# Attention and two MoE layers on one core: two staging buffers in turns, one weight block made early instead of two

## The chip, the core and the metric

The kernel runs on one core of a Trainium2 chip. TensorE (PE) multiplies matrices, VectorE (DVE), ScalarE (ACT) and GpSimd (POOL) work on elements, and SyncE (SP) issues the DMAs. The metric is the device time of one execution in microseconds (us), the median of several runs.

## The reference, cut to what matters

Attention with 16 heads in all (2 batches of 8), 768 tokens each, 64 wide: a query sees only keys whose nearest centroid (of 16) is the same as its own. Its output, 1536 tokens of 512, goes through two layers, each two dense products with an activation between:

```python
x = attn_out.transpose(0, 2, 1, 3).reshape(1536, 512)
h = x @ w_in;  g = maximum(0.01 * h, h);  x = g @ w_out        # layer 1 (m = 0)
h = x @ w_in2; r = maximum(h, 0); g = r * r; out = g @ w_out2  # layer 2 (m = 1)
```

w_in is 512 x 2048 and w_out 2048 x 512 in both. The weights arrive as 64-bit floats in HBM.

## The kernel before, in words

**Precision.** Every float32 operand is split into a high part and a low part, and a product is made of three matmuls: high by high, high by low, low by high. The names end in h and l: `xh`, `xl` (input of a layer), `wh`, `wl` (weights), `gh`, `gl` (activated rows).

**Weight blocks.** A layer's 2048 inner columns are cut into 16 blocks (f), so there are 32 blocks in all, numbered ci. A block holds 128 columns of w_in and 128 rows of w_out, 1 MB of 64-bit words. `decode_pieces` (L114) makes its `wh` and `wl` in six pieces: `load` (one DMA into `wraw`, L121), `mag` (ScalarE into `wt`, L128), `shift`, `low` and `sign` (VectorE on `wt` in place, L132, L138, L145; the last two also read `wraw`) and `split` (ScalarE copies `wt` to `wh`, L156, and GpSimd writes `wl` = `wt` - `wh`, L157). `wraw` and `wt` are staging: a pool `stg` with one of each, opened at the start of attention's last pair (L678), and a second pool `stgb` with one of each, opened when attention's pools are closed (L712). In the kernel before, `stg[-1]` is the pool opened last, so blocks 0 and 1 go through the first one and all others, one after the other, through the second. The finished blocks lie in a ring of eight.

**Attention.** Eight pairs of heads, six units to a pair, 48 in all. A unit is 256 query rows: scores S on TensorE (L350), row maxima on VectorE (L373), exponentials `e` on ScalarE (L383), division on GpSimd (L400), transposes T on TensorE (L413, twelve to a unit), their split `eh`, `el` (L424, L430), the product A with the values (L448, twelve matmuls), and `xt` (L461, L470). After the last unit of a pair `xsplit` writes `xh` and `xl` (GpSimd, L162 and L478).

**The layers.** A unit of a layer is one block of 512 tokens (b, three of them) and one weight block f: g1 is 12 matmuls into an `h` bank of PSUM (L725), in four row blocks of three; `act` makes `gh` and `gl` from it (L738 to L746); g2 is 12 matmuls into four `o` banks (L767), two units later (LAG). The first group has blocks 0 and 1, its units run (b0,f0), (b0,f1), (b1,f0), (b1,f1), (b2,f0), (b2,f1). Token block 0 needs only the first batch; token blocks 1 and 2 need, in the last of the four row blocks, the last pair of heads.

**Order.** SP's queue is in program order throughout. The other engines follow a list written out by hand up to unit 41; from the last pair on (L682) a planner orders each engine's instructions, with the program order as priority. The pieces of the early blocks are handed out over the six units of the last pair (L700 to L704); those of the others at units of the layers that `plan` names (L800 to L817): a block of group n is made while the group before it runs, and those of the first two groups at unit 0 and after it.

Of the kernel before, what the change touches and what calls it, by code (L numbers as in the profile page):

```python
# [10 lines left out]
I32 = mybir.dt.int32  # L11
# [41 lines left out]
def attention_moe_moe_kernel(  # L53
# [14 lines left out]
    NT, DM = out.shape  # L68
# [7 lines left out]
    NBLK = NT // N  # L76
    G = 4
    GROUPS = ([2, 2] + [G] * (NF // G - 1), [G] * (NF // G))
    EARLY = 2
    RING = 8  # L80
    WARM = (9,4,10)

# [29 lines left out]
    stg = []  # L112

    def decode_pieces(ci):  # L114

        m, f = divmod(ci, NF)
        st = {}

        def load():
            st["raw"] = stg[-1].tile([128, 2 * DM, 2], I32, tag="wraw", name="wraw")  # L120
            nc.sync.dma_start(  # L121
                out=st["raw"].rearrange("p a b -> p (a b)"), in_=(w1, w2)[m][f].bitcast(I32)
            )

        def mag():
            t = stg[-1].tile([128, 2 * DM], I32, tag="wt", name="wt")
            st["t"] = t
            nc.scalar.mul(out=t.bitcast(F32), in_=st["raw"][:, :, 1].bitcast(F32), mul=W_SHIFT)  # L128

        def shift():  # L130
            t = st["t"]
            nc.vector.tensor_scalar(  # L132
                out=t, in0=t, scalar1=3, scalar2=None, op0=ALU.logical_shift_left
            )

        def low():
            t = st["t"]
            nc.vector.scalar_tensor_tensor(  # L138
                out=t, in0=st["raw"][:, :, 0], scalar=29, in1=t,
                op0=ALU.logical_shift_right, op1=ALU.bitwise_or,  # L140
            )

        def sign():
            t = st["t"]
            nc.vector.scalar_tensor_tensor(  # L145
                out=t, in0=st["raw"][:, :, 1], scalar=-0x80000000, in1=t,
                op0=ALU.bitwise_and, op1=ALU.bitwise_or,
            )

        def split():  # L150
            t = st["t"].bitcast(F32)
            pool = next(q for q, n in ring if ci % RING < n)
            wh = pool.tile([128, 2 * DM], F32R, tag="wh", name="wh")
            wl = pool.tile([128, 2 * DM], F32R, tag="wl", name="wl")
            weights[m, f] = (wh, wl)
            nc.scalar.copy(out=wh, in_=t)  # L156
            nc.gpsimd.tensor_tensor(out=wl, in0=t, in1=wh.bitcast(F32), op=ALU.subtract)  # L157

        return [load, mag, shift, low, sign, split]

    def pool_copy(out, in_):
# [510 lines left out]
    }  # L672

    early = [f for i in range(EARLY) for f in decode_pieces(i)]
    for u in range(-1, NU + 5):
        if u == NU - UPP:
# [7 lines left out]
        for op in PLAN[FIRST[u] if p == 0 else u % UPP].split():  # L684
            if ":" in op:
                name, lag = op.split(":")
# [5 lines left out]
            else:  # L692
                name, ahead = op.split("@")
# [107 lines left out]
    for m in range(2):  # L801
        f = 0
        for g, size in enumerate(GROUPS[m]):
            for i in range(size):
                if ci >= EARLY:
                    pcs = decode_pieces(ci)
                    at = last + i * (began - last) // size
                    n = max((began - last) // size, 1)
                    for k, pc in enumerate(pcs):
                        plan.setdefault(at + k * n // len(pcs), []).append(pc)  # L810
                ci += 1
            last = began
            for b in range(NBLK):
                for i in range(size):
                    units.append((m, b, f + i, g, i == 0, i == size - 1))
            began = len(units)
            f += size  # L817
# [60 lines left out]
```

## Time and profile before

| | |
|---|---|
| median of 3 runs | 793.64 us (792.76 to 794.53) |
| the profiled execution | 790.98 us, span 789.2 us |
| PE busy | 771.2 us (98% of the span) |
| DVE, ACT, POOL busy | 538.0, 412.7, 292.0 us |
| granted TensorE clock | 1.00 of full speed |

The span is from the first to the last instruction. An engine's busy time is the union of its instructions; matmuls are pipelined, so a busy PE says that something was always in it, not that it was at its peak. A chain of waits is followed back from the last instruction to whatever released each step.

### The profile page before, as it was taken

The page shows a single profiled execution, that of the slowest core. Times are in us where ns is not written, and L with a number is a line of the kernel's source. Part 1 is how long each engine was busy: PE and PEld are TensorE (multiplying, and loading weights), DVE is VectorE, ACT ScalarE, POOL GpSimd, SP SyncE. Part 2 cuts the span into 40 slices and gives each one's busy share as a digit, 9 for nine tenths or more (in the row PEclk, how much of TensorE's full clock was granted, in tenths as well). Part 3 has the DMA queues.
Part 4 walks back from the last instruction along what each step waited for, and adds up shares of the span by engine and source line. Part 5 has one row for each costly group of instructions (what it writes and reads, how often), then busy time and mean ns, then how long its engine had stood idle before and what let it go on. Part 6 is the DMA issues. An engine that isn't in the chain of part 4 may idle for free.

```text
span 789.2 us, 11011 instructions
## 1 busy us (share of the span) xinstructions
PE 771.2 (98%) x4147; PEld 664.4 (84%) x4147; DVE 538.0 (68%) x772; ACT 412.7 (52%) x759; POOL 292.0 (37%) x257
## 2 busy tenths in 40 slices
PE   8999999999989999999999999999999999999998
PEld 8899999999977778888888888888888888888886
DVE  5899999999997378876665568387356547533333
ACT  6988988988996464443432344345344334222221
POOL 2989889888854322122220124352022012100000
PEclk9999999999999999999999999999999999999999
DMA  7584574564510323123221022013112103000102
GB/s 222 120 205 108 109 173 116 113 153 91 125 54 2 107 106 107 60 100 108 107 107 54 1 106 82 26 54 108 54 53 107 54 0 108 1 0 1 45 23 94
DMA packets 16005, 66.35 MB, mean 84 GB/s; under 512 B 2704, under 2 KB 2704, under 8 KB 10960
## 3 DMA queue, kind: packets, MB, share of 16 engines
q1 hardware_dynamic: 15952, 65.64, 28.7%
q8 instruction: 33, 0.54, 0.3%
q14 instruction: 20, 0.16, 0.1%
HBM read 44.60 MB, written 3.15 MB: 60 GB/s over the span
## 4 chain that ended last, share of the span: by engine, by line
PE 81%; DVE 11%; ACT 4%; DMA 1%; issue 1%; POOL 1%; SPq 0%; DVEq 0%; ACTq 0%
PE o L767 33%; PE h L725 33%; PE A L448 5%; PE T L413 5%; PE S L350 5%; DVE el L430 3%; DVE nm L373 3%; ACT e L383 2%; DVE xt L470 1%; ACT eh L424 1%; DVE ds L276 1%; PE ohT L305 1%; DVE m L275 1%; DMA rqk<-qk 1%; DVE wt L138 1%
## 5 line engine op out<-in xcount | busy, mean ns | idle before, releaser
L157 POOL TENSOR_TENSOR wl<-wt,wh 128x1024 fp32r<-128x1024 f32 x32 | 76.8, 2400 | 292.6 <-ACT wh L156 235.6
L725 PE MATMUL h<-xh,wh 128*128 128x512 f32 x384 | 150.6, 393 | 2.2 <-DVE g L739 2.2
L725 PE MATMUL h<-xh,wl 128*128 128x512 f32 x384 | 150.6, 392 | 0.0
L725 PE MATMUL h<-xl,wh 128*128 128x512 f32 x384 | 150.5, 392 | 0.0
L746 DVE TENSOR_TENSOR gl<-g,gh 128x512 fp32r<-128x512 f32 x96 | 95.4, 994 | 47.6 <-ACT gh L745 47.5
L430 DVE TENSOR_TENSOR el<-T,eh 128x512 fp32r<-128x512 f32 x144 | 94.8, 683 | 7.8 <-ACT eh L424 6.0
L745 ACT CAST gh<-g 128x512 fp32r<-128x512 f32 x96 | 59.6, 621 | 73.0 <-DVE g L742 42.7
L400 POOL TENSOR_SCALAR e<-e,r 128x768 f32<-128x768 f32 x96 | 88.0, 927 | 20.1 <-DVE r L397 14.7
L373 DVE TENSOR_REDUCE nm<-S 128x1 f32<-128x768 f32 x96 | 90.7, 946 | 4.6 <-PE S L254 2.2
L350 PE MATMUL S<-hb 128*128 128x384 f32 (+1 forms) x384 | 90.6, 350 | 3.0 <-ACT e L383 2.6
L383 ACT ACTIVATE e<-S,nm 128x768 f32<-128x768 f32 x96 | 87.0, 906 | 11.7 <-DVE nm L373 7.4
L742 DVE TENSOR_TENSOR g<-t 128x512 f32<-128x512 f32 x48 | 39.4, 822 | 72.8 <-ACT t L741 72.7
L725 PEld LDWEIGHTS h<-xh,wh 128*128 128x128 f32 x384 | 72.2, 188 | 18.5 <-DVE g L739 2.6
L741 ACT ACTIVATE t<-h 128x512 f32<-128x512 f32 x48 | 28.7, 598 | 112.0 <-PE h L725 111.9
L424 ACT CAST eh<-T 128x512 fp32r<-128x512 f32 x144 | 79.6, 585 | 12.9 <-PE T L413 12.3
L725 PEld LDWEIGHTS h<-xh,wl 128*128 128x128 f32 x384 | 72.2, 188 | 16.0
L725 PEld LDWEIGHTS h<-xl,wh 128*128 128x128 f32 x384 | 72.2, 188 | 15.9
L448 PE MATMUL A<-eh,vv 128*128 128x256 f32 x288 | 79.5, 306 | 3.5 <-DVE xt L470 3.5
L413 PE MATMUL T<-ident,e 128*128 128x128 f32 x576 | 81.0, 274 | 1.1 <-DVE el L430 1.0
L738 ACT ACTIVATE t<-h 128x512 f32<-128x512 f32 x48 | 28.6, 598 | 95.6 <-PE h L725 95.6
L767 PE MATMUL o<-gh,wl 128*128 128x512 f32 x192 | 75.3, 392 | 0.0
L767 PE MATMUL o<-gh,wh 128*128 128x512 f32 x192 | 74.5, 393 | 0.8 <-DVE xt L470 0.8
(105 smaller groups left out, 1454.0 us busy)
## 6 DMA issues: line engine op xcount, KB each, us to landing
wraw<-w SPq DMA_DIRECT2D x32, 1024.0 KB, 4.7
hb<-spl SPq DMA_DIRECT2D x14, 576.0 KB, 4.8
hb<-spl SPq DMA_DIRECT2D x42, 192.0 KB, 5.0
rqk<-qk SPq DMA_DIRECT2D x16, 384.0 KB, 4.5
rv<-v SPq DMA_DIRECT2D x8, 384.0 KB, 3.6
out<-ob SPq DMA_DIRECT2D x12, 256.0 KB, 2.1
twice<-qk SPq DMA_DIRECT2D x8, 192.0 KB, 6.4
hb<-st SPq DMA_DIRECT2D x28, 48.0 KB, 2.7
```

The source lines that it names most:

```text
L157: nc.gpsimd.tensor_tensor(out=wl, in0=t, in1=wh.bitcast(F32), op=ALU.subtract)
L350: nc.tensor.matmul(out=s[:, c, 0:HALF], lhsT=hb[0:k, a, i * 128 : (i + 1) * 128], rhs=hb[0:k, b, c * HALF : (c + 1) * HALF], start=(a == 0 ...
L373: nc.vector.tensor_reduce(out=n, in_=s_t[t][:, :, 0:HALF], axis=AX.XY, op=ALU.max, negate=True)
L383: nc.scalar.activation(out=e.rearrange("p (a b) -> p a b", a=2), in_=s_t.pop(t)[:, :, 0:HALF], func=AF.Exp, bias=n_t.pop(t), scale=1.0, ac ...
L400: nc.gpsimd.tensor_scalar(out=e_t[t], in0=e_t[t], scalar1=r_t[t // 2][:, t % 2 : t % 2 + 1], scalar2=1.0, op0=ALU.mult, op1=ALU.mult,)
L413: nc.tensor.transpose(T[:, o : o + 128], e_t[2 * u + b][:, kc * 128 : (kc + 1) * 128], ident)
L424: nc.scalar.copy(out=eh[:, 2 * g : 2 * g + 2, :].rearrange("p a b -> p (a b)"), in_=T_t[u, g])
L430: nc.vector.tensor_tensor(out=el[:, 2 * g : 2 * g + 2, :].rearrange("p a b -> p (a b)"), in0=T_t.pop((u, g)), in1=eh[:, 2 * g : 2 * g + 2, ...
L448: nc.tensor.matmul(out=A, lhsT=w, rhs=m[:, kc, :], start=(kc == 0 and i == 0), stop=(kc == KC - 1 and i == 1),)
L725: nc.tensor.matmul(out=h, lhsT=w[:, ws], rhs=x[:, kk, c], start=(kk == 0 and i == 0), stop=(kk == HP - 1 and i == 2),)
L746: nc.vector.tensor_tensor(out=gl, in0=g, in1=gh.bitcast(F32), op=ALU.subtract)
L767: nc.tensor.matmul(out=outs[o], lhsT=l, rhs=r, start=(first and i == 0), stop=(last and i == 2),)
```

## The change

Each block from the first that isn't made early takes the staging pool of its parity: even numbers the first, odd numbers the second. EARLY goes from 2 to 1: only block 0 is made inside attention's last pair, its six pieces one to a unit (before, twelve pieces, two to a unit). Block 1 is then planned as the other blocks are: `plan` puts all its six pieces at unit 0 of the layers, ahead of the first pieces of block 2.

```diff
-    EARLY = 2
+    EARLY = 1
...
         m, f = divmod(ci, NF)
         st = {}
+        own = ci % 2 if ci >= EARLY else 0
 
         def load():
-            st["raw"] = stg[-1].tile([128, 2 * DM, 2], I32, tag="wraw", name="wraw")
+            st["raw"] = stg[own].tile([128, 2 * DM, 2], I32, tag="wraw", name="wraw")
...
         def mag():
-            t = stg[-1].tile([128, 2 * DM], I32, tag="wt", name="wt")
+            t = stg[own].tile([128, 2 * DM], I32, tag="wt", name="wt")
```

## Rows read from the trace of the kernel before

**Rows 1.** By stretch: length; busy us of PE, PEld, DVE, ACT, POOL; clock, DMA share, GB/s.
```profile
132.00:158.00 26.00, 25.66 (x201) 24.97 (x200) 24.73 (x44) 22.98 (x53) 22.57 (x22) 1.00 0.57 121
213.40:245.06 31.66, 27.38 (x197) 24.77 (x196) 31.16 (x49) 27.94 (x60) 18.08 (x15) 1.00 0.10 34
245.06:275.90 30.84, 30.07 (x162) 25.03 (x160) 14.07 (x22) 14.72 (x26) 9.65 (x7) 1.00 0.20 70
275.90:278.08 2.18, 0.00 (x1) 0.00 (x0) 2.12 (x4) 0.90 (x3) 0.00 (x0) 1.00 0.00 0
278.08:785.40 507.32, 507.32 (x2208) 414.89 (x2208) 299.92 (x355) 186.74 (x275) 88.85 (x41) 1.00 0.18 63
```

**Rows 2.** Waits of SP's queue: who waited for whom, us in total, times, longest.
```profile
SPq L121 <- DVE wt L145: 382.0, 30, 34.6
...
SPq L121 <- PE T L413: 35.0, 1, 35.0
```

**Rows 3.** Timeline of DVE, last pair and seam: start, us, line, tiles, idle before.
```profile
222.97 1.20 DVE L145 SCALAR_TENSOR_TENSOR wt<-wraw,wt 128x1024 int32<-128x1024 int32 x1
...
231.38 0.68 DVE L132 TENSOR_SCALAR wt<-wt 128x1024 int32<-128x1024 int32 x1
...
233.35 1.21 DVE L138 SCALAR_TENSOR_TENSOR wt<-wraw,wt 128x1024 int32<-128x1024 int32 x1
...
236.55 2.55 DVE L145 SCALAR_TENSOR_TENSOR wt<-wraw,wt 128x1024 int32<-128x1024 int32 x1
...
267.49 0.43 DVE L470 TENSOR_TENSOR xt<-A,xt 64x256 f32<-64x256 f32 x1
```

**Rows 4.** Timeline of POOL, last pair.
```profile
236.20 1.82 POOL L478 TENSOR_TENSOR xl<-xt,xh 128x768 fp32r<-128x768 f32 x1
...
241.10 2.38 POOL L157 TENSOR_TENSOR wl<-wt,wh 128x1024 fp32r<-128x1024 f32 x1
```

**Rows 5.** Chain of waits across the seam: start, us, what.
```profile
243.79 1.43 PE A L448 x12
...
245.66 4.41 PE h L725 x19
...
259.08 0.45 PE T L413 x4
259.53 0.02 SPq L121
...
259.59 4.66 DMA wraw<-w
...
271.80 2.37 POOL wl L157
...
276.08 1.23 DVE wt L138
...
277.34 0.70 DVE g L739
```

**Rows 6.** Busy time by stretch of the matmuls of L725 alone.
```profile
245.06:259.20 14.14, 9.32 (x36) 6.62 (x36) 1.00 0.01 2
259.20:275.90 16.70, 9.09 (x36) 6.64 (x36) 1.00 0.36 127
```

**Rows 7.** Timeline of ACT at the seam.
```profile
264.33 1.14 ACT L128 ACTIVATE wt<-wraw 128x1024 f32<-128x1024 f32 x1 [4.19 <-DMA wraw<-w]
...
269.21 1.05 ACT L156 CAST wh<-wt 128x1024 fp32r<-128x1024 f32 x1 [2.75 <-DVE wt L145]
```

**Rows 8.** The issue of L190 at 126.8, and its landing.
```profile
L190 SPq DMA_DIRECT2D rqk<-qk x1: 588/588/588, 126.8 to 126.8; - x1
...
DMA to landing us min/median/max: 4.6/4.6/4.6
```

**Rows 9.** The issue of L191 at 127.5, and its landing.
```profile
L191 SPq DMA_DIRECT2D rqk<-qk x1: 462/462/462, 127.5 to 127.5; - x1
...
DMA to landing us min/median/max: 4.9/4.9/4.9
```

## The prediction

> **What bounds the kernel now.** Read the table of busy time by stretch first [rows 1], then SP's waits [rows 2], the timelines of VectorE and GpSimd [rows 3, 4], and last the chain of waits across the seam between attention and the first product [rows 5]. The table shows four regimes. In a steady pair of heads TensorE is busy 25.66 of 26.00 us. In attention's last pair (213.40 to 245.06) it is busy only 27.38 of 31.66 us, while VectorE is busy 31.16: there VectorE sets the pace. Over the seam (245.06 to 275.90) TensorE is busy 30.07 of 30.84 us, filling attention's waits with 72 matmuls of the first layer, and then it idles 2.18 us. From 278.08 to 785.40 it is busy 507.32 of 507.32 us with 2208 matmuls, 0.230 us each. So in 507 us of the 789.2 us span nothing but TensorE counts, and the change can be worth something only in the last pair and at the seam. The page's own execution took 790.98 us (span 789.2 and 1.8 around it), 2.66 below the median of 793.64; I sum differences and add them to the median.
>
> **Alternating buffers in the long stretch: 0.** What the second buffer takes away there is SP waiting for L145 before the next load (382.0 us in 30 waits [rows 2]) and ScalarE waiting to overwrite `wt`. Both lie beside a TensorE with no idle time [rows 1]. What it adds, loads and VectorE pieces that come sooner, goes into the same cover; VectorE is busy 299.92 of those 507.32 us. If a piece of 1.2 us comes ahead of an activation, TensorE has the two units of lag, some 5.5 us of matmuls (24 at 0.230), before it is late. Taken 0; I bound it by -0.3 and +0.5, about a quarter of the one stall of this kind that the trace has (2.18).
>
> **Attention's last pair: -3.5.** Block 1's pieces leave it: on VectorE 0.68 + 1.21 + 2.55 = 4.44 us (L132, L138, L145 [rows 3]), on GpSimd 2.38 [rows 4], on ScalarE two instructions of about 1.1 (the same two for block 2 stand in [rows 7]). VectorE's 31.16 falls to 26.72, and TensorE's 27.38 becomes the floor: the gain is at most 31.66 - 27.38 = 4.28. At the steady pair's share (25.66/26.00) it is 31.66 - 27.74 = 3.9. Against it: the 2.55 us L145 started at 236.55, inside GpSimd's two-input `xl` of 236.20 to 238.02; block 0's, at 222.97 without one, took 1.20. With half the pieces per unit, block 0's sign piece is now handed out at the end of the very unit that hands out that `xl`, so the 1.35 us may come back: VectorE 28.07, and at its present share (31.16/31.66) 28.5 us, a gain of 3.1. At VectorE's steady share (24.73/26.00) it is 29.5, a gain of 2.2. Taken 3.5, between the second and third; ends 2.2 and 4.3. Block 0 itself is finished later than now, where block 1 is finished now (its `wl` ends at 243.48 [rows 4], 1.9 us ahead of the first matmul of the layer at about 245.4): hidden.
>
> The Trainium skill, "SBUF — State Buffer", section "Who interferes with whom", says that a VectorE instruction with two SBUF inputs contends with a GpSimd instruction that reads SBUF, and that the one issued second is blocked until the first has finished. The pair of L145 durations above agrees (1.20 without, 2.55 beside `xl`), and by that rule alone the gain would be the 3.1 of the third case.
>
> **The seam: +2.4.** Block 1 now goes into the second buffer, which lies on memory that attention's `e` tiles hold. The trace shows when that comes free: today's third load (block 2, the first into that buffer) waited 35.0 us for a transpose L413 [rows 2], and was issued at 259.53, as the last four transposes ended [rows 5]. After the change block 1's load stands there, and it is issued ahead of block 2's on SP's queue, so its decode starts when attention is nearly over, not inside it. Behind the waiting load SP has only the loads of blocks 2, 3 and on; block 2's, whose buffer has long been free, is held up with it, and ScalarE's mag of block 1 and TensorE's f=1 units wait for the chain. Step by step, on today's time axis (the shift of 3.5 comes off at the end):
>
> The last transpose: ahead of it stand 36 of the layer's matmuls, behind it another 36 [rows 6]. Those that need no block 1 and no last pair number 12 + 9 + 9 = 30 (token block 0, and three of the four row blocks of the token blocks 1 and 2). With 30 instead of 36 it ends 6 x 0.230 = 1.4 earlier, at 258.1.
>
> Block 1 is ready: block 2's own row today gives 4.66 for the load [rows 5], then from 264.33 to 269.21 + 1.05 for mag, three VectorE pieces and `wh` [rows 7], less the 0.43 of `xt` L470 that stood between them [rows 3], that is 10.3 from issue to `wh`; `wl` takes 2.37 more [rows 5], since GpSimd will be done with the last `xh` and `xl`. So `wh` at 258.1 + 10.3 = 268.4 and `wl` at 270.8.
>
> What TensorE has meanwhile: attention's last 12 products (1.43 [rows 5]), 12 matmuls of g2 for unit 0 and 6 of the last row block, 18 x 0.230 = 4.1. It is through by about 264, and idles until 268.4. Then two matmuls for each of three units (1.4), and idle again until 270.8. By then 30 + 12 + 6 + 6 = 54 of the 96 matmuls are done that today are done at 275.90 (72 and 24 of g2); the other 42 take 9.7, to 280.5. Today the next one starts at 278.08. Cost 280.5 - 278.08 = +2.4; if the two matmuls are not put ahead, +3.3.
>
> Today's 2.18 us stall: TensorE waited for a PSUM bank of `h` that L739 had to read, and VectorE had L132 and L138 of block 3 ahead of it until 277.31 [rows 5]; block 3 began at 274.17 because `wl` of block 2 held the one `wt`. That wait goes: block 2 has its own buffer. What is late next is `wl` of block 1, and it is in the sum. Three blocks (1, 2, 3) are now decoded between 263 and 280 where two were, 3.1 us of VectorE each, beside the activations of block 1's units: a stall of that kind may come back, 0 to 2.2; taken 0.7, a third of the row.
>
> **Sum.** -3.5 + 2.4 + 0.7 + 0 = -0.4 us: 793.64 - 0.4 = 793.2. That is no change that a measurement of this kernel can tell (0.2% is 1.6 us).
>
> **Rivals.**
>
> Faster, the starvation is smaller than I think: the order of TensorE is planned anew, and with fewer of the layer's matmuls available the planner may put the last transposes ahead of them. Were all 36 behind, the last transpose would end at 259.53 - 36 x 0.230 = 251.3 and `wl` be ready at 264, just when the other work runs out: no idle time, and the 42 matmuls end at 273.7, so 4.4 ahead of 278.08 and with the 3.5 up to 7.9 faster. For it: the 36 in front of the last transpose [rows 6] are the planner's choice. Against: it is the same planner, and the first 19 [rows 5] have ready weights in both kernels. A third of the way there is about -2.7: 790.9.
>
> Slower, two loads share the engines: today no two weight loads fly together, since each waits for L145. Block 2's load is now issued 0.33 behind block 1's. If the engines share evenly, block 1 lands up to 4.3 us later, and all of it is idle TensorE: -0.4 + 4.3 = +3.9, 797.5; it decides from 2.0 us of delay. Against: the paired loads of 384 KB, issued 0.7 apart, land 4.6 and 4.9 after issue [rows 8, 9], so at 131.4 and 132.4, one after the other.
>
> The Trainium skill, "DMA: Bandwidth & Descriptors", section "Queues, rings and completion order", says that on each DMA engine descriptors are consumed in ring order; by that rule block 1 keeps its 4.66 and this rival is void. The pair of landings agrees as far as it goes.
>
> Slower, both halves at their bad ends: VectorE in the last pair only at its steady share (gain 2.2, not 3.5) and the activations again late by the whole 2.18: -2.2 + 2.4 + 2.2 = +2.4, 796.0. For it: 31.16 of 31.66 was reached with more pieces to choose from. It decides from 1.6.
>
> **Chances.** My forecast (791.9 to 795.2, within 0.2%) 0.43; the faster rival 0.33; shared loads 0.10; both bad ends 0.14. So faster 0.33, same 0.43, slower 0.24. The range runs from 790.2, which holds the faster rival to some four tenths of its way, to 796.6, which holds the bad ends and leaves out shared loads.
>
> **What would show it.** Right: SP's wait of L121 for L413 is now before the second load; a busy TensorE of some 27.4 in a last pair of about 28; TensorE idle 5 us in all before its first matmul with block 1, waiting for `wl` L157; no wait for L739 after it; 2208 matmuls again in 507 us. Wrong: a last pair still of 31 us (something other than VectorE's pieces set it); no idle time at the seam; idle TensorE in the long stretch; block 1's load taking over 5.5 us.

## The result, and the profile after

The changed kernel takes 800.3 us (median of 4, 799.91 to 800.93) against 793.6 (792.76 to 794.53): a ratio of 1.0094, 95% interval 1.0082 to 1.0106, so 6.7 us slower. 793.2 was predicted, with a range up to 796.6. The profiled execution took 800.93 us, with a span of 799.1 and a mean granted clock of 0.993. Lines stand one lower than before (L122 loads, L129 is mag, L133, L139 and L146 are VectorE's pieces, L157 and L158 make `wh` and `wl`).

First the table by stretch, which answers [rows 1] (columns: length; busy us of PE, PEld, DVE, ACT, POOL with instructions; clock, DMA share, GB/s). The first line is the last pair, the next two the seam, the fourth a part of the third, and the last a stretch that reaches into what was the steady regime:

```profile
213.76:241.40 27.64, 26.33 (x199) 25.13 (x198) 27.23 (x47) 25.94 (x58) 16.49 (x15) 1.00 0.00 1
...
250.00:260.00 10.00, 5.18 (x28) 3.71 (x26) 5.12 (x8) 3.84 (x6) 2.67 (x2) 0.93 0.54 210
260.00:270.00 10.00, 9.16 (x30) 7.35 (x31) 7.75 (x5) 3.17 (x4) 5.35 (x2) 0.73 0.59 210
...
261.00:265.20 4.20, 4.20 (x10) 3.31 (x11) 3.85 (x2) 0.28 (x1) 2.81 (x1) 0.50 0.61 238
...
272.00:312.00 40.00, 34.66 (x148) 26.99 (x146) 39.03 (x33) 24.75 (x38) 15.39 (x6) 1.00 0.46 158
```

The last pair is 4.0 us shorter (27.64 after 31.66). But from 272 to 312 VectorE is busy 39.03 of 40 us, and TensorE idles 5.3 us there; before, from 278.08 on, it idled not at all [rows 1]. What TensorE waited for (waiting line, releaser, us in total, times, longest):

```profile
PE h L726 <- ACT wh L157: 5.0, 1, 5.0
PE h L726 <- DVE g L740: 3.1, 1, 3.1
...
PE o L768 <- DVE gl L747: 2.1, 1, 2.1
```

The first is the seam, one wait for block 1. The other two are waits for activations on VectorE; before there was one such wait, of 2.18 us. From 320 to 720 TensorE is busy all but 0.15 us, at 0.230 us per matmul, as before: the lost time lies between 250 and 320 us.

SP's waits, which answer [rows 2]: the wait for the transpose now stands before block 1's load, and that for `wt` L146 has shrunk from 382.0 to 354.1 us. The loads do come sooner: block 10's is issued at 304.8 us, in the kernel before at 343.1.

```profile
SPq L122 <- DVE wt L146: 354.1, 29, 48.8
...
SPq L122 <- PE T L414: 41.4, 1, 41.4
```

The chain across the seam, which answers [rows 5] (start, us, what), and the two loads issued back to back at its head (issue rows of L122, then their landing in us, minimum, median, maximum):

```profile
250.43 0.02 SPq L122
...
250.49 4.77 DMA wraw<-w
...
255.34 1.13 ACT wt L129
```

```profile
L122 SPq DMA_DIRECT2D wraw<-w x2: 334/350/367, 250.5 to 250.9; - x2
...
DMA to landing us min/median/max: 4.8/5.8/6.8
```

The first load lands in 4.8 us, the second in 6.8, some 2.4 behind it: the first is hardly slowed by the second (4.66 alone in the kernel before [rows 5]). The Trainium skill, "DMA: Bandwidth & Descriptors", section "Queues, rings and completion order", says that each DMA engine consumes its descriptors in ring order; the trace agrees.

VectorE's timeline answers [rows 3] (start, us, line, operation, tiles, idle before):

```profile
223.32 1.21 DVE L146 SCALAR_TENSOR_TENSOR wt<-wraw,wt 128x1024 int32<-128x1024 int32 x1
...
267.04 1.96 DVE L133 TENSOR_SCALAR wt<-wt 128x1024 int32<-128x1024 int32 x1 [2.15 <-ACT wt L129]
269.03 1.23 DVE L139 SCALAR_TENSOR_TENSOR wt<-wraw,wt 128x1024 int32<-128x1024 int32 x1
270.29 1.22 DVE L146 SCALAR_TENSOR_TENSOR wt<-wraw,wt 128x1024 int32<-128x1024 int32 x1
271.44 0.69 DVE L133 TENSOR_SCALAR wt<-wt 128x1024 int32<-128x1024 int32 x1
272.16 1.22 DVE L139 SCALAR_TENSOR_TENSOR wt<-wraw,wt 128x1024 int32<-128x1024 int32 x1
273.42 3.27 DVE L146 SCALAR_TENSOR_TENSOR wt<-wraw,wt 128x1024 int32<-128x1024 int32 x1
276.72 1.29 DVE L740 TENSOR_TENSOR g<-h,t 128x512 f32<-128x512 f32 x2
```

Two blocks' pieces stand back to back from 267.04 to 276.69, and the activation that TensorE waits for (L740) comes behind them. The last L146 takes 3.27 us instead of 1.22, beside the `wl` that GpSimd has been at since 272.68.

Last TensorE after its wait (start, us, line; the distance of the starts counts):

```profile
264.84 0.63 PE L726 MATMUL h<-xl,wh 128*128 128x512 f32 x1
265.27 0.49 PE L726 MATMUL h<-xh,wl 128*128 128x512 f32 x1
265.60 0.39 PE L726 MATMUL h<-xh,wh 128*128 128x512 f32 x1
265.83 0.39 PE L726 MATMUL h<-xl,wh 128*128 128x512 f32 x1
```

For some 4.4 us the matmuls are 0.427 us apart, then 0.23: the granted clock is 0.50 there, its lower level, 1.2 GHz, right after the idle 5.0 us. It happens again from 313.4 to 316.7 (0.51), after the wait of 2.1. After the wait of 3.1 it does not: from 272 to 312 the clock is 1.00.

### The profile page after: what moved, and what is told of

It reads as the page before. It is cut to its first block, busy times and chain, and to the rows that moved or that the text cites. A ratio compares the mean times of both kernels' runs of the same rounds, so it can differ in the third digit from the quotient of the medians.

```text
span 799.1 us, 11034 instructions
## 1 busy us (share of the span) xinstructions
PE 775.8 (97%) x4147; PEld 667.8 (84%) x4147; DVE 551.4 (69%) x772; ACT 411.9 (52%) x759; POOL 299.0 (37%) x257
## 4 chain that ended last, share of the span: by engine, by line
PE 74%; DVE 18%; ACT 4%; issue 2%; DMA 1%; POOL 0%; DVEq 0%; ACTq 0%; SPq 0%; POOLq 0%
PE o L768 29%; PE h L726 28%; PE A L449 5%; PE S L351 5%; PE T L414 5%; DVE el L431 4%; DVE nm L374 3%; DVE wt L139 2%; DVE wt L146 2%; ACT e L384 1%; DVE wt L133 1%; DMA wraw<-w 1%; DVE gl L747 1%; DVE xt L471 1%; PE warm L200 1%
## 5 line engine op out<-in xcount | busy, mean ns | idle before, releaser
L158 POOL TENSOR_TENSOR wl<-wt,wh 128x1024 fp32r<-128x1024 f32 x32 | 87.3, 2728 | 283.8 <-ACT wh L157 253.0
L746 ACT CAST gh<-g 128x512 fp32r<-128x512 f32 x96 | 59.7, 622 | 101.6 <-DVE g L743 57.8
L747 DVE TENSOR_TENSOR gl<-g,gh 128x512 fp32r<-128x512 f32 x96 | 76.0, 792 | 41.8 <-ACT gh L746 41.1
L742 ACT ACTIVATE t<-h 128x512 f32<-128x512 f32 x48 | 28.6, 597 | 105.8 <-PE h L726 105.8
L768 PE MATMUL o<-gl,wh 128*128 128x512 f32 x192 | 76.3, 397 | 2.2 <-DVE gl L747 2.1
L768 PE MATMUL o<-wh,gl 128*128 128x512 f32 x192 | 75.4, 393 | 0.1
```

Of the source, the lines that this page charges most:

```text
L747: nc.vector.tensor_tensor(out=gl, in0=g, in1=gh.bitcast(F32), op=ALU.subtract)
L768: nc.tensor.matmul(out=outs[o], lhsT=l, rhs=r, start=(first and i == 0), stop=(last and i == 2),)
```

## The experiments

### Which part of the change costs the time

Turns alone (`e1`): EARLY stays 2, the pools alternate from block 2 on. One early block alone (`e2`): EARLY is 1, all later blocks go through the second pool.

```diff
# e1                                       # e2
-    EARLY = 1                             -        own = ci % 2 if ci >= EARLY else 0
+    EARLY = 2                             +        own = 1 if ci >= EARLY else 0
```

> Buffers in turns, but blocks 0 and 1 still made inside attention's last pair. Theory A (the late block 1 alone makes the changed kernel slower): no wait of TensorE for wh L157, 793.6 or less, down to 791.5 as the 2.2 us stall of before goes. Theory B (the turns alone: pieces of two blocks crowd VectorE ahead of the activations): about 800, with waits of TensorE for L740 or L747 of some 5 us in all and half clock after them. Both, each by the stalls read in the changed kernel's trace (3.1 + 2.1 us of waits and 1.7 of half clock, less the 2.95 of idle time of before): about 797.5.

> Only block 0 made early, but all other blocks one after the other through the second pool, as before. Theory A: about 800 (the wait for wh of 5.0 us and the half clock after it are there, and they are the whole loss). Theory B: 793.6 or less, since attention ends 4.0 us sooner and the turns are gone. Both: -4.0 + 5.0 + 2.0 on 793.6, so about 796.6, with no wait of TensorE for L747.

Turns alone: 799.77 us (799.02 to 799.84) beside 793.03 of the kernel before, a ratio of 1.0085 (1.0070 to 1.0100). One early block alone: 792.74 (791.5 to 793.97), 0.9998 (0.9988 to 1.0007). The turns carry the whole loss. In turns alone TensorE has one wait of over 1 us behind attention, and after it the lower clock (waits, then the stretch by columns as above):

```profile
PE h L726 <- DVE g L740: 6.7, 1, 6.7
```

```profile
280.00:290.00 10.00, 6.25 (x15) 4.95 (x16) 9.65 (x9) 5.91 (x10) 3.77 (x2) 0.51 0.48 179
```

Its VectorE and ScalarE show what was ahead of that activation:

```profile
270.20 1.32 DVE L133 TENSOR_SCALAR wt<-wt 128x1024 int32<-128x1024 int32 x1
271.56 2.76 DVE L139 SCALAR_TENSOR_TENSOR wt<-wraw,wt 128x1024 int32<-128x1024 int32 x1
274.35 3.31 DVE L146 SCALAR_TENSOR_TENSOR wt<-wraw,wt 128x1024 int32<-128x1024 int32 x1
...
283.01 1.29 DVE L740 TENSOR_TENSOR g<-h,t 128x512 f32<-128x512 f32 x2
```

```profile
277.69 1.04 ACT L157 CAST wh<-wt 128x1024 fp32r<-128x1024 f32 x1 [4.23 <-DVE wt L146]
...
279.12 1.13 ACT L129 ACTIVATE wt<-wraw 128x1024 f32<-128x1024 f32 x1
...
280.62 1.09 ACT L739 ACTIVATE t<-h 128x512 f32<-128x512 f32 x2
```

Block 2, whose load no longer waits for attention's end, was made among attention's last units (its L146 at 249.81); block 3's pieces begin at 266.62, and block 4's, shown here, follow without a gap. ScalarE's queue holds block 4's `wh` (which waits 4.23 us for L146) and the mag of the next block ahead of `t` L739, and VectorE's holds two pieces of that next block ahead of `g` L740. TensorE stood from 277.0 to 283.75. Against before: 6.75 - 2.18 = 4.6 us of idle time, and some 13 matmuls 0.427 instead of 0.230 apart, 2.6 us; 7.2 of the 8.8 us between the two profiled spans. Of the other 1.6, 1.1 lies ahead of the seam: the load that waits for the last transpose is issued at 260.70, before at 259.59 [rows 5].

### Is it the stretched pieces, or their order?

The pieces are stretched where GpSimd's `wl` runs beside them. Two kernels take `wl` out of GpSimd's reads in `e1`: `wl` on VectorE (`e5`), or filled with zeros by GpSimd, which then reads nothing (`e6`; the low part of the weights is left out).

```diff
-            nc.gpsimd.tensor_tensor(out=wl, in0=t, in1=wh.bitcast(F32), op=ALU.subtract)
+            nc.vector.tensor_tensor(out=wl, in0=t, in1=wh.bitcast(F32), op=ALU.subtract)   # e5
+            nc.gpsimd.memset(wl.bitcast(F32), 0.0)                                         # e6
```

> Buffers in turns with two early blocks, and wl made on VectorE in place of GpSimd. Theory P (the loss of the turns comes from GpSimd's wl of one block blocking VectorE's two-input pieces of the next): pieces back to 0.7 and 1.2 us, no wait over 2.5 us for L740, 791 to 794. Theory O (the order: two blocks' pieces stand ahead of the activations): VectorE gets some 1.2 us more per block in the same place, the wait of 6.7 us stays or grows, 799 to 803.

> As e1, but GpSimd fills wl with zeros, which reads nothing, instead of wt - wh (left out: the low part of the weights, so the result differs). Theory P: the blocked time of VectorE in e1's stall (1.32, 2.76, 3.31 us where 0.69, 1.23, 1.22 are normal: 4.3 us in sum) is gone, the wait for L740 falls from 6.7 to about 2.4, the half clock behind it goes: 793 or less. Theory O: the pieces still stand ahead of the activations, wait of 5 us or more, 797 to 800.

799.47 us (ratio 1.0085, 1.0070 to 1.0100) and 799.95 (1.0095, 1.0075 to 1.0115), beside 792.93: no better than turns alone in the whole. But these two runs don't settle it. The wait for L740 falls from 6.7 to 3.5 us in `e5` and 4.2 in `e6`, and both lose time elsewhere: their load that waits for the last transpose is issued at 263.74 and 263.64, in `e1` at 260.70. From there to the end of the span they need 534.0 and 534.7 us, `e1` 537.3 and the kernel before 529.6. So 3.3 and 2.6 of the 7.7 us that `e1` loses behind the seam are gone, and 3.0 are lost ahead of it. Nor is all stretching gone, since `xl` reads beside the pieces too; in `e6`:

```profile
275.26 2.69 POOL L479 TENSOR_TENSOR xl<-xt,xh 128x768 fp32r<-128x768 f32 x1
```

```profile
276.28 2.75 DVE L146 SCALAR_TENSOR_TENSOR wt<-wraw,wt 128x1024 int32<-128x1024 int32 x1
```

So the stretching may have a share in the loss; how much, and how much is left to the order alone, the pieces that stand ahead of the activations, is not shown.

Single staging until block 3, turns from block 4 on (`e8`, from `e1`), asks whether it is only the seam:

```diff
-        own = ci % 2 if ci >= EARLY else 0
+        own = (ci % 2 if ci >= 4 else 1) if ci >= EARLY else 0
```

> As e1, but blocks 2 and 3 go one after the other through the second pool as before; turns begin with block 4. If the loss belongs to the seam (blocks 2, 3 and 4 decoded while attention's last outputs and the first activations want VectorE): 793 to 794.5, one wait of 2.2 us as before. If the turns cost wherever two blocks overlap: waits for L740 or L747 move to 290 to 320 us, 796 to 800.

796.16 us, 1.0045 (1.0031 to 1.0059). The wait for L740 is 2.2 as in the kernel before, but VectorE is as full 40 us later, and TensorE stands there (2.1 us in three waits for `acc` L784, where VectorE adds an `o` bank to the running sum of the second products):

```profile
310.00:320.00 10.00, 8.78 (x37) 6.57 (x36) 9.93 (x11) 4.67 (x6) 3.48 (x2) 1.00 0.44 157
```

So the turns cost in either place: in `e1` at the seam, here 40 us later, 3.2 us instead of 6.7.

### Which of the two tiles

The staging has two tiles. Only `wraw` in turns (`e10`), or only `wt` (`e10b`), both from `e1`:

```diff
-            t = stg[own].tile([128, 2 * DM], I32, tag="wt", name="wt")
+            t = stg[-1].tile([128, 2 * DM], I32, tag="wt", name="wt")                      # e10
...
-            st["raw"] = stg[own].tile([128, 2 * DM, 2], I32, tag="wraw", name="wraw")
+            st["raw"] = stg[-1].tile([128, 2 * DM, 2], I32, tag="wraw", name="wraw")       # e10b
```

> The first two blocks as in the kernel before; only the load buffer (wraw) goes in turns, the decode tile (wt) stays single. Theory O (two blocks' pieces reach VectorE back to back, ahead of the activations; the single wt is what keeps them apart): within 1.5 us of the kernel before, 792 to 794.5, and the wait for g L740 at the seam 1.5 to 3 us as before, with the granted clock near 1.00 after it. Rival (the earlier loads and their place in memory cost the time): 798 to 800 as with both tiles in turns, a wait of 5 us or more.

> The first two blocks as in the kernel before; only the decode tile (wt) goes in turns, the load buffer (wraw) stays single, so a block's load still waits for the sign piece of the block before. Theory O: pieces of two blocks can't be back to back, since a load of about 5 us lies between them; 792 to 795, no TensorE wait over 3 us at the seam. Rival (the second wt alone lets pieces pile up): 797 to 800.

`wraw` alone: 789.3 us (788.58 to 790.31), 0.9957 (0.9943 to 0.9970), faster than the kernel before, which had not been expected. `wt` alone: 792.79, 0.9998 (0.9987 to 1.0010). Neither tile loses by itself; both together lose 6.7. With one `wt`, mag of the next block must wait for `wl` of the last; with one `wraw`, its load of 4.7 us must wait for L146. Either keeps two blocks' pieces apart. VectorE with `wraw` alone in turns:

```profile
262.36 0.70 DVE L133 TENSOR_SCALAR wt<-wt 128x1024 int32<-128x1024 int32 x1 [0.34 <-ACT wt L129]
...
264.35 1.23 DVE L146 SCALAR_TENSOR_TENSOR wt<-wraw,wt 128x1024 int32<-128x1024 int32 x1
...
270.34 2.08 DVE L133 TENSOR_SCALAR wt<-wt 128x1024 int32<-128x1024 int32 x1 [2.28 <-ACT wt L129]
...
273.72 1.23 DVE L146 SCALAR_TENSOR_TENSOR wt<-wraw,wt 128x1024 int32<-128x1024 int32 x1
276.55 1.29 DVE L740 TENSOR_TENSOR g<-h,t 128x512 f32<-128x512 f32 x2 [1.61 <-ACT t L739]
```

Five us lie between the two blocks, and the activation is on time: TensorE waits 1.2 us. Block 3 is ready earlier than in the kernel before (its L133 at 270.34, there 275.35): its mag waits for block 2's `wl` in both, and block 2's load, now into the first buffer, no longer waits for attention's end (issued at 240.3, there at 259.6 [rows 5]).

Does the same hold in the change itself, with one early block? The change with the single `wt` (`e13`):

```diff
-            t = stg[own].tile([128, 2 * DM], I32, tag="wt", name="wt")
+            t = stg[int(ci >= EARLY)].tile([128, 2 * DM], I32, tag="wt", name="wt")
```

> The change itself, but only the load buffer (wraw) goes in turns; the decode tile (wt) of all blocks from the second on is single. Theory (it is the second wt that lets two blocks' pieces pile up): TensorE's wait of 5.0 us for wh of block 1 and the half clock after it stay, the wait of 2.1 for gl goes, VectorE in 272 to 312 is busy under 9 of 10 us, and the time is 790 to 793, like one early block alone (792.7) or a little better. Rival (the seam of one early block costs more of its own once a load may come earlier): 796 to 800.

792.96 us beside 793.29, 0.9995 (0.9986 to 1.0004): one tile less in turns, and the 6.7 us are gone. TensorE's only new wait is 4.9 us for block 1. The groups of VectorE's instructions between 255 and 320 us say why (line, operation, tiles, count | busy us, mean ns of one | idle before); first the change, then `e13`:

```profile
L146 DVE SCALAR_TENSOR_TENSOR wt<-wraw,wt 128x1024 int32<-128x1024 int32 x10 | 16.3, 1634 | 0.3
L139 DVE SCALAR_TENSOR_TENSOR wt<-wraw,wt 128x1024 int32<-128x1024 int32 x10 | 16.0, 1601 | 0.2
L133 DVE TENSOR_SCALAR wt<-wt 128x1024 int32<-128x1024 int32 x11 | 13.2, 1197 | 5.2 <-ACT wt L129 5.2
L747 DVE TENSOR_TENSOR gl<-g,gh 128x512 fp32r<-128x512 f32 x8 | 8.5, 1077 | 1.9 <-ACT gh L746 1.9
L740 DVE TENSOR_TENSOR g<-h,t 128x512 f32<-128x512 f32 x9 | 6.0, 684 | 0.3
```

```profile
L747 DVE TENSOR_TENSOR gl<-g,gh 128x512 fp32r<-128x512 f32 x11 | 9.4, 851 | 7.9 <-ACT gh L746 7.9
L146 DVE SCALAR_TENSOR_TENSOR wt<-wraw,wt 128x1024 int32<-128x1024 int32 x7 | 8.6, 1222 | 0.1
L139 DVE SCALAR_TENSOR_TENSOR wt<-wraw,wt 128x1024 int32<-128x1024 int32 x7 | 8.5, 1220 | 0.1
L740 DVE TENSOR_TENSOR g<-h,t 128x512 f32<-128x512 f32 x11 | 7.5, 687 | 5.2 <-ACT t L739 5.0
L133 DVE TENSOR_SCALAR wt<-wt 128x1024 int32<-128x1024 int32 x7 | 4.9, 694 | 9.5 <-ACT wt L129 9.5
```

In the same 65 us the change decodes 10 blocks where `e13` decodes 7, each at a higher price, 45.5 us of pieces against 22.0, and gets fewer activations done (9 and 8 against 11 and 11). The free buffers let the decoding run ahead, on the engine that the activations need. At `e13`'s mean times the change's 31 pieces would take 32.1 us: of the 23.5 more, 10.1 are more pieces and 13.4 their stretching.

### Can the planner be told, and what is the seam worth?

The activations of the first product with a high priority (`e11`, from `e1`):

```diff
-            pend.append((*units[U], *act(m, g1(m, b, f))))
+            h = g1(m, b, f)
+            with tc.high_priority():
+                pend.append((*units[U], *act(m, h)))
```

> Both tiles in turns from the first block on, and the activations of the first product are given to the planner with a high priority. Theory O in the form that the planner's order is chosen by priority: the wait of 6.7 us for g L740 falls under 3 us, 793 to 796. In the form that the order follows the planner's own times, in which the pieces are ready before the activations: no change, 799 to 800, the wait 6 to 7 us.

799.98 us, 1.0097 (1.0067 to 1.0127), the same wait of 6.7, and VectorE's pieces and activations in the same order at the seam: no help.

Three kernels change what may run before block 1 is ready. `e3` (from the change) and `e9` (from `e2`) put the f=0 units of all three token blocks first; `e4` (from the change) adds one matmul with block 0's weights that opens the `h` bank of unit (b0,f1), so that this unit counts as begun.

```diff
+    seq = [0, 2, 4, 1, 3, 5] + list(range(6, len(units)))                 # e3, e9
...
+        if (m, b, f) == (0, 0, 1):                                        # e4
+            nc.tensor.matmul(out=h, lhsT=weights[0, 0][0][:, 384:512],
+                             rhs=xh[:, HP - 1, S : S + N], start=True, stop=True)
```

> The changed kernel, with the g1 of the first group issued in the order b0f0, b1f0, b2f0, b0f1, b1f1, b2f1 (g2 in the old order), so that 24 matmuls that need no block 1 stand ahead of the wait for it. Theory A: the wait of 5.0 us for wh falls under 1 us, the half clock behind it goes (2.0), and the kernel is 5 to 7 us faster than the changed one: 793.5 to 795.5. Theory B: the VectorE crowd behind it takes back what is won, within 2 us of the changed kernel's 800.3.

> The changed kernel with one extra matmul of block 0's weights into the h bank of unit b0f1 ahead of its own twelve, which start the bank afresh: the result is unchanged, one matmul of 0.23 us is added. If the planner holds back a unit's matmuls until the unit before it in program order has begun (order rival to: the later units were simply not ready), the twelve matmuls of b1f0 now run before the wait for wh: the wait falls from 5.0 to about 2, the half clock behind it is shorter or gone, and the kernel is 2.5 to 4.5 us faster than 800.3. If they were not ready, nothing moves: 800 to 801.

> Block 0 alone early, no turns, and the first group's g1 in the order b0f0, b1f0, b2f0, b0f1, b1f1, b2f1. The early half of the change lost a wait of 5.0 us for wh and half clock after it to the order of the units and won it back from attention's end. With the order mended both may stand: wait for wh under 2 us, no half clock, 787 to 789.5, faster than before. If the wait only moves behind the 24 matmuls: 791 to 793.

`e3`: 797.78 us, 1.0062 (1.0047 to 1.0077), with waits of 3.2 us in all for `gl` L747. `e4`: 797.29, 1.0052 (1.0037 to 1.0067); the 12 matmuls of (b1,f0) now run before the wait, which falls from 5.0 to 1.9 us, and other waits grow (`acc` 2.4 and 1.3, L740 1.3). `e9`: 791.44, 0.9979 (0.9970 to 0.9989); in `e3` and `e9` 30 of the layer's matmuls run ahead of the last transpose, in the change 12, and the wait is 3.2. So the seam's idle time depends on what the planner may start; by `e4` it starts (b1,f0) only once the unit ahead of it has begun.

Then smaller first groups, [1, 1, 2] instead of [2, 2]: from `e2` (`e12`), from `e13` (`e14`), from `e10` (`e15`).

```diff
-    GROUPS = ([2, 2] + [G] * (NF // G - 1), [G] * (NF // G))
+    GROUPS = ([1, 1, 2] + [G] * (NF // G - 1), [G] * (NF // G))
```

> One block inside the last pair, all later ones in the single second buffer, and the first groups of token blocks 1, 1, 2 instead of 2, 2. Theory of the seam (TensorE waits 5.0 us for wh of block 1 because only 12 + 12 matmuls may run before it): the first token block's units then run in another order; if that leaves more work ahead of block 1, the wait is under 2 us, the clock stays near 1.00 and the time is 787 to 790. If the wait stays at 4 to 5 us: 791 to 793. If the small groups cost more in accumulations than they give: 794 to 797.

> As the last, and the first groups of token blocks 1, 1, 2. If the seam's wait and the pile of pieces are separate terms, the time is that of small first groups alone (789.4) less what the load buffer's turns give, 787 to 789.5, with no TensorE wait over 2.5 us. If not: 790 or more.

> Two blocks early as before, only the load buffer in turns (789.3), and the first groups 1, 1, 2. If the smaller groups help only where one block is early: 789 to 792. If they help by more work ahead of the first activations: 787 to 789.

`e12`: 789.44 us, 0.9957 (0.9941 to 0.9974); the wait for `wh` is 0.4, and one of 2.2 us for `gh` L746 is new (2.5 in `e14`). `e14`: 789.63, 0.9954 (0.9941 to 0.9966), no better than `e12` or `e10`: the gains do not add. `e15`: 793.23, 1.0003 (0.9993 to 1.0014): with two early blocks small groups undo what `wraw` in turns gives; a wait of 2.0 us for `xl` L479 is new. (Two of the expectations say "of token blocks"; the groups are of weight blocks.) Three kernels beat the kernel before by some 3.5 us, and the change by about 10: `e10`, `e12` and `e14`.

## Why the prediction was wrong, point by point

**Alternating buffers in the long stretch: 0, bounds -0.3 and +0.5. This is the step that failed.** Turns alone cost 6.7 us, and with a single `wt` the loss is gone (`e10`, `e13`). I argued from an average: VectorE is busy 299.92 of 507.32 us [rows 1], and a piece of 1.2 us ahead of an activation is covered by two units of lag, 5.5 us. Both numbers stand, but not one piece comes ahead of an activation: some ten us of pieces of two blocks do, single ones stretched to 3.3 us, and ScalarE's queue is held with them. What I read as a wait that costs nothing (SP for L145, 382.0 us [rows 2]) and the wait for the one `wt` were the brake that kept the decoding at the pace of the activations; one of the two is brake enough (`e10`, `e10b`, `e13`). I had named ScalarE's wait for `wt` but not what it held back. In `e1` the loss stands where today's stall stood, in the change partly there and partly at 312, inside the long stretch (2.1 us of wait, 1.5 of lower clock).

**Today's 2.18 us stall may come back: +0.7, at most 2.2.** The same cause, mis-sized: in the change the two waits on VectorE are 3.1 and 2.1 us, and 1.5 us of lower clock follows the second (8 gaps in 3.37 us, from 313.38 to 316.75, instead of 8 x 0.230). That is 6.7 of the 8.4 us between the profiled spans of the change (799.1) and of one early block alone (790.7). I had counted three blocks' pieces at 3.1 us each; the blocks that followed them weren't counted at all.

**Attention's last pair: -3.5, bounds 2.2 and 4.3.** Right: -4.0. VectorE is busy 27.23 us, between my 26.72 and 28.07, and still sets the pace; TensorE's own work there is 26.33. Block 0's L146 took 1.21 us at 223.32, ahead of `xl` (233.87): the collision for which I had left 1.35 us didn't come.

**The seam: +2.4.** The size is near, the working doesn't hold. One early block alone, which is this and the last term, measured -0.3 (792.74 beside 793.03) where the two terms give -1.1; with the last pair at -4.0 that leaves +3.7 for the seam. The chain is as I wrote it: wait for the transpose, load 4.77 (predicted 4.66), `wh` 10.3 us after the last transpose (250.43 to 260.78; predicted 10.3). But the last transpose ended 4.2 us earlier than I had it (250.43 against 258.1 - 3.5 = 254.6), since TensorE had only 12 of the layer's matmuls ahead of it, not 30: the planner holds (b1,f0) until (b0,f1) has begun (`e4`). Where 30 do run ahead of it, in `e3` and `e9`, it ends at 253.4 and 254.1. So block 1 came earlier by as much as the work ahead of it was shorter, and the idle time came out at the 5 us I had named. It waited for `wh`, not, as I had it, in the end for `wl`. Not in the sum at all was the lower clock after it: 11 gaps in 4.76 us (260.84 to 265.60) instead of 2.5, 2.2 us.

**The rivals.** Two loads sharing the engines: void, they land one after the other. The faster one: TensorE did put the last transposes earlier, but the matmuls that would have covered the load couldn't start. Both halves at their bad ends: the stalls on VectorE were there, larger than its end of 2.2, while the last pair was near its good end. I had no rival in which the turns themselves cost more than half a microsecond, and the range could not hold one.

## What to carry to other kernels

A single buffer between two engines is also a throttle. Before a second one is added, ask who shares an engine with the work that it lets run ahead, and look at that engine in the first stretch where both are there, not at an average: VectorE, busy 59% of 507 us before, was busy 98% of the 40 us from 272 to 312 after. If only the transfer is to come sooner, double the tile that the transfer fills and keep the next one single: here that gave 3.4 us with two early blocks and nothing with one.

## What the runs showed of the hardware that was not expected

The lower clock cost 2.2, 1.5 and 2.6 us after waits of 5.0, 2.1 and 6.7, and nothing after the change's wait of 3.1: the length of a wait alone doesn't tell. It would account for most of the 2.66 us between the profile of the kernel before and its median. Of the 67 executions of that kernel beside these runs, 4 had a mean granted clock of 1.000 and took 791.1 to 791.9 us (median 791.3); 54 had 0.998 and took 791.9 to 794.1 (median 793.2). The profile shown was one of the few at 1.000. Of the others there is no trace, but `wt` alone in turns has the same wait, at a clock of 0.998, and its trace shows what they may do after it:

```profile
278.12 0.51 PE L726 MATMUL h<-xh,wh 128*128 128x512 f32 x1 [2.14 <-DVE g L740]
278.47 0.47 PE L726 MATMUL h<-xl,wh 128*128 128x512 f32 x1
278.74 0.63 PE L726 MATMUL h<-xh,wl 128*128 128x512 f32 x1
279.16 0.63 PE L726 MATMUL h<-xh,wh 128*128 128x512 f32 x1
```

After nearly the same wait (2.14 and 2.18 us) the clock is soon at 1.2 GHz here, 0.427 us apart until 281.72, and stays at 2.4 GHz in the profile before [rows 1]. In `e10`, with a wait of 1.2, all 8 executions had a clock of 1.000; by the two groups above, some 1.9 of its 3.4 us would be the clock (an estimate from 793.2 - 791.3).

L133 has one input, and it too was held by GpSimd: 0.69 us alone, 1.96 at 267.04 beside the `wl` of 266.05. The Trainium skill, "SBUF — State Buffer", section "Who interferes with whom", says that a TENSOR_SCALAR in its two-port mode takes the shared pair of ports and is blocked by whoever was first; the trace agrees, and L133 alone takes 0.69 us against 1.22 of L139, both 128x1024, which would fit such a mode; no row names the mode.
